# A Fourier transform feeding a mixture of experts: mirrored columns folded in the tables for five batches instead of three, and two batches' row tails written by VectorE

## The chip, the cores and the metric

The kernel runs on one core of a Trainium2 chip. The metric is the device time of one execution in microseconds (us). The kernel before has a median of 1130.99 us over three runs (1129.47 to 1132.53).

## The reference

The input x has 8 batches of 2496 rows with 256 features. The reference takes the Fourier transform over the rows and over the features and keeps the real part. Each of the 19968 resulting rows then goes to one of 8 experts:

```
X = np.fft.fft(x, axis=1);  X = np.fft.fft(X, axis=2);  x = X.real
logits = x @ w_gate;  e_idx = np.argmax(logits, axis=1)
gate_w = probs[np.arange(N), e_idx]              # softmax over the experts
eom = 1 / (1 + np.exp(-(x @ w_output_gate)))
for e in range(E):
    h = np.maximum(x[mask] @ w1[e], 0)           # 256 -> 1024
    out[mask] = gate_w * eom[mask, e] * (h @ w2[e])   # 1024 -> 256
```

So there is a transform of all batches, a gating decision per row, and two matrix products per row with the weights of its expert.

## The kernel before

**The transform of a batch.** A batch comes in five chunks of up to 128 columns (tiles `xt`, 128 x 8 x 128, fp32). `fold1` adds one half of a chunk to the other half (L416). For the batches from `LB` on it makes two more sums of the mirrored columns (L419, L420); for batches below `LB` it stops after L416, and the tables take that fold over. `fold2`, on VectorE (DVE), makes the tile `ft` (L431, L434, L443, L445). `dstage` multiplies a chunk with the first transform's tables, in fp32, for two parities: below `LB` as two accumulated products with 290 columns (L485), from `LB` on as three smaller products with 145, 80 and 145 columns (L487 to L489). `devac` rounds the result into the fp16 pair `ahi` and `alo` (ScalarE, ACT, at L497; DVE at L498). `sstage` is the second transform (fp16, L524), in five steps i for each batch; `sevac` adds and splits its result into `rows` (L546 to L559), tiles whose rows hold 256 features and two more words.

**Gating.** `gating(b)` picks the expert of each row and its place in a table in HBM, `scr`. It ends by writing two words, weight and place, behind the features of the rows: five small copies on ACT (L653). Then come 20 indirect DMAs (L657), issued by GpSimd (POOL), which scatter the rows into `scr`. They are woven in groups of five (`SPL`) between the chunks' folds.

**The experts.** They start when batches 0 and 1 have been scattered (`BA` = 2). A slot takes 256 rows of one expert: `load_x_` reads `scr` through a transposing DMA (L1105, tile `xr`) and a small DMA (L1106), both issued by SP; `conv` makes fp16 pairs of the weights (L1125, L1126); `mm1` and `mm2` are the two products (L1145 into `hp`, L1165 into `yp`); L1149 and L1150 evacuate `hp` into `hh` and `hl`; L1172 scales the result and L1173 (POOL) writes it out. The transform of the later batches runs in between.

**Who does fold1, and the order.** Chunks of batches 0 and 1 have their `fold1` on DVE, all others on POOL. SP and POOL run their instructions in the order in which the program is written; PE (TensorE), ACT and DVE in an order that a scheduler chose when the kernel was built. Each engine takes its queue strictly in order.

Of the kernel before, what the change touches and what calls it, by code (L numbers as in the profile page):

```python
# [12 lines left out]
I32 = mybir.dt.int32  # L13
# [4 lines left out]
NB, S, D, E, F = 8, 2496, 256, 8, 1024  # L18
# [16 lines left out]
RW = D + 2  # L35
# [6 lines left out]
BA = BAS[0]  # L42
# [28 lines left out]

AHEAD = (5, 6, 7, 8, 9), (4, 5, 6, 7, 8)

LB = BA + 1
PH1 = {mybir.EngineType.SP, mybir.EngineType.Pool}
BIG = float(1 << 20)

# [155 lines left out]
def fft_moe_kernel(ctx: ExitStack, tc: tile.TileContext, xl, wg, w1, w2, tde, tdo, gt, ts0, tsm, tsr, tsq, cst, tid, out):  # L233
    nc = tc.nc
# [43 lines left out]
    if True:  # L278
# [129 lines left out]
        def fold1(b, c, eng):  # L408
# [7 lines left out]
            eng.tensor_tensor(x0, x0, x1, op=ALU.add)  # L416
            if b < LB:
                return
# [3 lines left out]
        def fold2(b, c):  # L422
# [5 lines left out]
            ft = f[c] = pf.tile([128, 2, 2, 128], F32, name="ft", tag="ft", bufs=7)  # L428
            h = int(b >= LB)
            v = xts[b, c].rearrange("p (h a b) n -> p h a b n", h=2, a=2)[:, h]  # L430
# [45 lines left out]
        def dstage(b, c):  # L476
# [4 lines left out]
            for par in range(2):  # L481
                o = ps[W, par]
                if b < LB:
                    for k in range(2):
# [76 lines left out]
        def gating(b):  # L561
# [11 lines left out]
            def t3(name, shape=(128, 20, 8)):  # L573
                return pg.tile(list(shape), F32, name="r_" + name, tag="r_" + name, bufs=1)
# [70 lines left out]
            car = t3("car", (128, 20, 2))  # L645
# [4 lines left out]
            for i in range(5):  # L650
                r_ = s["rows"][i].rearrange("p a d w -> p (a d) w")
                rf.append(r_)
                nc.scalar.copy(r_[:, :, D:RW].bitcast(I32), car[:, 4 * i:4 * i + 4].bitcast(I32))  # L653
                yield

            def scatter(j):
# [326 lines left out]
        def steps():  # L983
            wk = 0
            fc = KC + 1
            for n in range(5 * NB):
                b, i = divmod(n, 5)
                if i == 0 and b > 0:
                    add_gen(gating(b - 1))
                    if b <= BA:  # L990
                        for ph in "CACC":
                            weave(piece(ph))
                    if b == BA:
                        first.append(table_a(0))
                        while next(first[0]) != "scales":
                            pass
# [30 lines left out]
                while wk <= 2 * E and wk < (n + 1) * (2 * E + 1) / WEND:  # L1027
# [5 lines left out]
                    wk += 1  # L1033
                yield ("step", n)
            add_gen(gating(NB - 1))
            while gens:
                for _ in piece("C"):
# [293 lines left out]
```

## Time and profile before

| what | value |
|---|---|
| median of the runs shown | 1130.99 us |
| the profiled execution: time, and its span | 1137.68 us, 1135.9 us |
| mean granted TensorE clock | 0.976 of full speed |
| PE busy | 1044.0 us (92% of the span) |
| DVE busy | 822.9 us (72%) |
| ACT busy | 732.4 us (64%) |
| POOL busy | 490.1 us (43%) |
| chain that ended last, by engine | PE 63%, POOL 9%, DVE 8%, issue 7%, ACT 7%, DMA 4% |

Busy shares are means over stages. The page's 40 slices (28.4 us each) show PE at 4 to 5 tenths in the third to sixth slice and at 9 or more almost everywhere from the twelfth on, while POOL is at 8 tenths in the fourth to sixth slice, its highest. So the stages must be read apart. The first number of a row of the timeline is its start within the span, the second how long it took; in brackets stands how long the engine idled before it and what ended that.

### The profile page before, as it was taken

The numbers are of one execution on the slowest core, as the hardware profiler recorded it, in microseconds if no ns is written. First come the engines' busy times: TensorE is split into PE (matmuls) and PEld (weight loads), VectorE is DVE, ScalarE is ACT, GpSimd is POOL, SyncE is SP. The second block draws the span as 40 slices with busy tenths as digits, with TensorE's granted clock in tenths as the row PEclk, the third lists the DMA queues.
The fourth block names the chain that finished last, engine by engine and source line by source line (L and its number), as shares of the span: only waits on it lengthen the run. The fifth ranks groups of instructions, "written<-read, shape, count | busy, mean of one in ns | idle before, by whom it ended". The sixth has DMA issues, their size and how long they took to land.

```text
span 1135.9 us, 28531 instructions
## 1 busy us (share of the span) xinstructions
PE 1044.0 (92%) x10060; PEld 932.3 (82%) x10060; DVE 822.9 (72%) x1516; ACT 732.4 (64%) x1224; POOL 490.1 (43%) x417
## 2 busy tenths in 40 slices
PE   5874559979889999999999999999999999999898
PEld 4664549869779899998888888899889989898787
DVE  6768877786988857578544545587788777787684
ACT  3887547656676655655445455677777776787584
POOL 0238874848848455463762122132222222322231
PEclk9998759989999999999999999999999999999999
DMA  9886545655558556667876424647667555565651
GB/s 369 318 312 232 216 122 180 176 157 162 164 147 187 154 135 164 157 170 184 208 195 167 109 57 140 177 136 176 163 168 200 133 167 126 140 183 137 182 131 30
DMA packets 158212, 194.08 MB, mean 171 GB/s; under 512 B 117885, under 2 KB 118527, under 8 KB 156020
## 3 DMA queue, kind: packets, MB, share of 16 engines
q1 hardware_dynamic: 142100, 149.68, 49.4%
q0 software_dynamic: 15824, 42.14, 11.2%
q8 instruction: 79, 1.29, 0.5%
q14 instruction: 65, 0.53, 0.2%
q10 hardware_dynamic: 144, 0.44, 0.1%
HBM read 193.47 MB, written 43.46 MB: 209 GB/s over the span
## 4 chain that ended last, share of the span: by engine, by line
PE 63%; POOL 9%; DVE 8%; issue 7%; ACT 7%; DMA 4%; SPq 2%; POOLq 0%; DVEq 0%; ACTq 0%
PE hp L1145 30%; PE yp L1165 29%; POOL scr L657 4%; PE psb_t L524 2%; POOL xt L416 2%; POOL out_dram L1173 2%; ACT wt L369 1%; DVE w1b L1126 1%; DVE w0b L1126 1%; DMA raw1b<-in_w_dram 1%; DVE hl L1150 1%; ACT w1b L1125 1%; DMA scr<-rows,desti 1%; DMA wt<-in_w_dram 1%; POOL xt L420 1%
## 5 line engine op out<-in xcount | busy, mean ns | idle before, releaser
L1145 PE MATMUL hp<-xr,w0b 128*128 128x256 f16 (+2 forms) x4224 | 484.2, 265 | 25.2 <-DVE hl L1150 18.6
L1165 PE MATMUL yp<-w1b,hh 128*128 128x256 f16 x2608 | 448.0, 273 | 3.7 <-DVE w1b L1126 2.1
L1145 PEld LDWEIGHTS <-w0b 128*128 128x128 f16 x4224 | 385.9, 98 | 76.1 <-issue 16.3
L1173 POOL DMA_INDIRECT out_dram<-y,xf x163 | 213.4, 1309 | 522.6 <-ACT y L1172 490.5
L1165 PE MATMUL yp<-w1b,hl 128*128 128x256 f16 (+3 forms) x1304 | 355.8, 273 | 0.0
L1165 PEld LDWEIGHTS <-hh 128*128 128x128 f16 x2608 | 251.5, 98 | 32.0 <-issue 3.9
L1149 ACT ACTIVATE hh<-hp 128x512 f16<-128x512 f32 (+4 forms) x352 | 193.9, 554 | 116.8 <-PE hp L1145 116.2
L1150 DVE SCALAR_TENSOR_TENSOR hl<-hp,hh 128x512 f16<-128x512 f32 (+4 forms) x352 | 222.4, 638 | 58.6 <-ACT hh L1149 57.8
L1126 DVE SCALAR_TENSOR_TENSOR w1b<-raw1b,ssc,w1b 128x1024 f16<-128x1024 f32 x144 | 188.0, 1307 | 104.1 <-ACT w1b L1125 104.1
L1126 DVE SCALAR_TENSOR_TENSOR w0b<-raw0b,ssc,w0b 128x1024 f16<-128x1024 f32 x144 | 188.4, 1311 | 63.2 <-ACT w0b L1125 60.7
L657 POOL DMA_INDIRECT scr<-rows,desti x160 | 183.7, 1148 | 67.7 <-issue 44.2
L1125 ACT ACTIVATE w0b<-raw0b,ssc 128x1024 f16<-128x1024 f32 x144 | 164.5, 1146 | 64.3 <-PE hp L1145 40.2
L1125 ACT ACTIVATE w1b<-raw1b,ssc 128x1024 f16<-128x1024 f32 x144 | 165.0, 1147 | 48.1 <-PE yp L1165 34.8
L1165 PEld LDWEIGHTS <-hl 128*128 128x128 f16 (+3 forms) x1304 | 127.8, 98 | 17.4 <-issue 2.5
L1172 ACT ACTIVATE y<-yp,ysc 128x256 f32<-128x256 f32 (+1 forms) x163 | 68.9, 470 | 47.8 <-PE yp L1165 41.7
L416 POOL TENSOR_TENSOR xt<-xt 128x500 f32<-128x500 f32 (+1 forms) x30 | 40.6, 1354 | 48.2 <-DMA xt<-in_xl_dram 27.2
L524 PE MATMUL psb_t<-ahi,tstq 125*128 125x145 f16 (+1 forms) x384 | 42.4, 230 | 0.3 <-DVE alo L498 0.3
L485 PE MATMUL psb_t<-tdet,ft 128*125 128x290 f32 (+1 forms) x120 | 34.4, 440 | 8.9 <-DVE alo L498 5.1
L524 PEld LDWEIGHTS <-tstq 125*128 125x128 f16 (+1 forms) x576 | 39.9, 99 | 1.9 <-issue 0.6
L487 PE MATMUL psb_t<-tdet,ft 128*125 128x145 f32 (+1 forms) x100 | 23.1, 315 | 17.1 <-DVE eo L548 10.6
L524 PE MATMUL psb_t<-alo,tstq 125*128 125x145 f16 (+1 forms) x192 | 38.6, 228 | 0.0
L555 DVE TENSOR_TENSOR rows<-rt,rows 128x516 f16<-128x516 f32 x40 | 31.5, 789 | 9.1 <-ACT rows L554 8.8
(213 smaller groups left out, 867.2 us busy)
## 6 DMA issues: line engine op xcount, KB each, us to landing
raw0b<-in_w_dram SPq DMA_DIRECT2D x144, 512.0 KB
raw1b<-in_w_dram SPq DMA_DIRECT2D x144, 512.0 KB
xt<-in_xl_dram SPq DMA_DIRECT2D x40, 512.0 KB
wt<-in_w_dram SPq DMA_DIRECT2D x16, 1024.0 KB
out_dram<-y,xf POOLq DMA_INDIRECT x163, 3.3
scr<-rows,desti POOLq DMA_INDIRECT x160, 4.9
xr<-scr SPq DMA_TRANSPOSE x88
xf<-scr SPq DMA_DIRECT2D x75, 2.0 KB
```

What stands on the lines that cost most here:

```text
L416: eng.tensor_tensor(x0, x0, x1, op=ALU.add)
L485: nc.tensor.matmul(o[:, 0:290], ft[:, k, par, W], tdab[:, k], start=(k == 0), stop=(k == 1))
L524: nc.tensor.matmul(ps[:, k, c0:c0 + 145], tab[hl][t][K], a[K, kc, par, c0:c0 + 145], start=(n == 0), stop=(n == len(terms) - 1))
L657: free_order("scr", batch=b, inst=nc.gpsimd.indirect_dma_start(out=scr[:, :], out_offset=bass.IndirectOffsetOnAxis(ap=desti[:, j:j + 1], a ...
L1125: nc.scalar.activation(w[:, 0], r, AF.Copy, scale=sc)
L1126: nc.vector.scalar_tensor_tensor(w[:, 1], r, sc, w[:, 0], op0=ALU.mult, op1=ALU.subtract)
L1145: nc.tensor.matmul(ps[:, k, T], w1v[:, hl, kc, (f % 4) * 128:(f % 4 + 1) * 128], a["x"][:, x, T], start=(m == 0), stop=(m == 5))
L1149: nc.scalar.activation(hh[:, G, T], ps[:, :, T], AF.Relu)
L1150: nc.vector.scalar_tensor_tensor(hl[:, G, T], ps[:, :, T], 0.0, hh[:, G, T], op0=ALU.max, op1=ALU.subtract)
L1165: nc.tensor.matmul(a["yp"][0:M, u], a[k, h][:, f, u * 128:u * 128 + M], w2v[:, hl, f], start=(g == 0 and f == 0 and m == 0), stop=(h == 1 ...
L1172: nc.scalar.activation(a["y"][0:M, u], a["yp"][0:M, u], AF.Copy, scale=ys[0:M, u:u + 1])
L1173: free_order("out", nc.gpsimd.indirect_dma_start(out=out[:, :], out_offset=bass.IndirectOffsetOnAxis(ap=a["f"].bitcast(I32)[0:M, u, 1:2], ...
```

## The change

`LB` goes from 3 to 5: `fold1` ends after L416 for batches 3 and 4 too, and their `dstage` takes the two products with 290 columns. In `gating`, for batches 0 and 1, the five copies of weight and place are made by DVE instead of ACT. Line numbers behind that place grow by 3 (L657 is L660 in the changed kernel, L1145 is L1148).

```
-LB = BA + 1
+LB = BA + 3
...
-                nc.scalar.copy(r_[:, :, D:RW].bitcast(I32), car[:, 4 * i:4 * i + 4].bitcast(I32))
+                if b < BA:
+                    nc.vector.tensor_copy(r_[:, :, D:RW].bitcast(I32), car[:, 4 * i:4 * i + 4].bitcast(I32))
+                else:
+                    nc.scalar.copy(r_[:, :, D:RW].bitcast(I32), car[:, 4 * i:4 * i + 4].bitcast(I32))
```

Place one, POOL, from the first scatters of batch 0 on (`xt` is a chunk, `scr` the table in HBM). Before:

```order
L657 DMA scr<-rows,desti 161024x258 x5
L416 TENSOR_TENSOR xt<-xt 128x4x125
L419 TENSOR_TENSOR xt<-xt 128x2x125
L420 TENSOR_TENSOR xt<-xt 128x2x125
L416 TENSOR_TENSOR xt<-xt 128x4x125
L419 TENSOR_TENSOR xt<-xt 128x2x125
L420 TENSOR_TENSOR xt<-xt 128x2x125
L657 DMA scr<-rows,desti 161024x258 x5
L416 TENSOR_TENSOR xt<-xt 128x4x125
```

Of the change, the same place on POOL:

```order
L660 DMA scr<-rows,desti 161024x258 x5
L416 TENSOR_TENSOR xt<-xt 128x4x125 x2
L660 DMA scr<-rows,desti 161024x258 x5
L416 TENSOR_TENSOR xt<-xt 128x4x125
L660 DMA scr<-rows,desti 161024x258 x5
```

The L419 and L420 of ten chunks are gone, eight of these chunks ahead of the last scatter of batch 1; nothing else of POOL's or SP's order is different.

Place two, DVE, where the gating of batch 0 ends (`r_car` holds weight and place, `alo` is the first transform's low half). Before:

```order
L647 SCALAR_TENSOR_TENSOR r_car<-r_se,p_x,r_num 128x20
L498 SCALAR_TENSOR_TENSOR alo<-psb_t,p_x,ahi 125x580 x2
L542 SCALAR_TENSOR_TENSOR rt<-psb_t,qb 128x2x129 x2
L555 TENSOR_TENSOR rows<-rt,rows 128x4x129
L498 SCALAR_TENSOR_TENSOR alo<-psb_t,p_x,ahi 125x580 x2
L548 SCALAR_TENSOR_TENSOR eo<-psb_t,qb 128x290 x2
L431 TENSOR_TENSOR ft<-xt 128x2x125
```

Of the change, the same place on DVE:

```order
L647 SCALAR_TENSOR_TENSOR r_car<-r_se,p_x,r_num 128x20
L498 SCALAR_TENSOR_TENSOR alo<-psb_t,p_x,ahi 125x580
L654 COPY rows<-r_car 128x4x2 x5
L498 SCALAR_TENSOR_TENSOR alo<-psb_t,p_x,ahi 125x580
L542 SCALAR_TENSOR_TENSOR rt<-psb_t,qb 128x2x129 x2
L555 TENSOR_TENSOR rows<-rt,rows 128x4x129
L498 SCALAR_TENSOR_TENSOR alo<-psb_t,p_x,ahi 125x580
L431 TENSOR_TENSOR ft<-xt 128x2x125
L434 TENSOR_TENSOR xt<-xt 128x2x125
L431 TENSOR_TENSOR ft<-xt 128x2x125
```

The five copies stand behind one L498, and the first fold of batch 3 (L431) stands earlier among the other work.

Place three, PE, just ahead of the experts' first product (`hp`). Before:

```order
L487 MATMUL psb_t<-tdet,ft 125x145
L488 MATMUL psb_t<-tdot,ft 125x80
L489 MATMUL psb_t<-tdot,ft 125x145
L600 MATMUL psm_t<-r_inc,cs 128x8
L601 MATMUL psm_t<-r_inc,cs 128x8
L1145 LDWEIGHTS w0b_1528
L1145 MATMUL hp<-xr,w0b_1528 128x256
```

Of the change, the same place on PE:

```order
L524 LDWEIGHTS tst_108
L524 MATMUL psb_t<-ahi,tst_108 128x145
L524 LDWEIGHTS tst_108
L524 MATMUL psb_t<-alo,tst_108 128x145
L1148 LDWEIGHTS w0b_1510
L1148 MATMUL hp<-xr,w0b_1510 128x256
```

The last 19 products (L524) of batch 3's first step, the first transform of two chunks of batch 4 and the two small products of batch 2's gating (L600, L601), which stood ahead of the experts' first 24 products, now stand behind them. On DVE, 24 instructions that stood ahead of the first L1150 stand behind it: two L548, two L552, two L555 and 18 of batch 2's gating.

## Rows read from the trace of the kernel before

**Rows 1.** Windows: stretch, length, busy PE, PEld, DVE, ACT, POOL; clock, DMA, GB/s

```profile
75.00:155.60 80.60, 43.76 (x407) 40.63 (x407) 60.90 (x163) 50.75 (x99) 69.03 (x64) 0.77 0.58 205
140.00:170.00 30.00, 14.77 (x75) 12.23 (x75) 22.15 (x57) 14.71 (x38) 22.87 (x21) 0.60 0.43 115
170.00:200.00 30.00, 30.00 (x305) 27.65 (x306) 22.60 (x37) 20.84 (x34) 14.03 (x12) 1.00 0.59 180
```

**Rows 2.** Chain that ended last, 140 to 182 us: start, length, what

```profile
161.29 3.55 DMA xf<-scr
```

**Rows 3.** Timeline of PE, 153 to 162 us: the experts' first product

```profile
160.55 1.87 PE L1145 MATMUL hp<-xr,w0b 128*128 128x256 f16 x8 [5.77 <-DMA xr<-scr]
```

**Rows 4.** Groups of POOL, 74 to 155.7 us: busy, mean ns | idle before

```profile
L657 POOL DMA_INDIRECT scr<-rows,desti x40 | 46.8, 1169 | 32.9 <-ACT rows L653 22.1 <-issue 10.2 <-ACT ahi L497 0.6
...
L420 POOL TENSOR_TENSOR xt<-xt 128x250 f32<-128x250 f32 (+1 forms) x8 | 6.4, 796 | 0.0
L419 POOL TENSOR_TENSOR xt<-xt 128x250 f32<-128x250 f32 (+1 forms) x8 | 6.3, 789 | 0.6
```

**Rows 5.** Timeline of POOL, 74 to 156 us

```profile
74.75 1.14 POOL L657 DMA_INDIRECT scr<-rows,desti  x1 [22.07 <-ACT rows L653]
...
82.36 0.72 POOL L419 TENSOR_TENSOR xt<-xt 128x250 f32<-128x250 f32 x1
...
104.50 1.27 POOL L416 TENSOR_TENSOR xt<-xt 128x500 f32<-128x500 f32 x1
...
117.61 1.17 POOL L657 DMA_INDIRECT scr<-rows,desti  x1 [0.16 <-issue]
...
154.63 0.99 POOL L657 DMA_INDIRECT scr<-rows,desti  x1 [0.30 <-issue]
```

**Rows 6.** Timeline of DVE, 70 to 101 us

```profile
70.45 0.23 DVE L647 SCALAR_TENSOR_TENSOR r_car<-r_se,p_x,r_num 128x20 f32<-128x20 f32 x1
70.60 1.55 DVE L498 SCALAR_TENSOR_TENSOR alo<-psb_t,p_x,ahi 125x580 f16<-125x580 f32 x2
...
93.70 0.33 DVE L585 SCALAR_TENSOR_TENSOR r_score<-r_dd,cs 128x160 f32<-128x160 f32 x1
...
100.67 0.23 DVE L647 SCALAR_TENSOR_TENSOR r_car<-r_se,p_x,r_num 128x20 f32<-128x20 f32 x1
100.82 0.17 DVE L754 CAST r_av<-r_pri 128x8 f32<-128x8 int32 x1
100.89 0.17 DVE L629 TENSOR_TENSOR desti<-r_dest,cs 128x20 int32<-128x20 f32 x1
```

**Rows 7.** Timeline of ACT, 74 to 75 us

```profile
74.25 0.61 ACT L653 COPY rows<-r_car 128x8 int32<-128x8 int32 x5
```

**Rows 8.** Timeline of PE, 33 to 94 us: first transform, both forms

```profile
33.69 4.13 PE L485 MATMUL psb_t<-tdet,ft 128*125 128x290 f32 x16
...
92.59 0.41 PE L487 MATMUL psb_t<-tdet,ft 128*125 128x145 f32 x2
...
93.30 0.41 PE L487 MATMUL psb_t<-tdet,ft 128*125 128x145 f32 x2
```

**Rows 9.** Chain that ended last, 322 to 330 us

```profile
324.32 1.91 PE psb_t L524 x30
```

**Rows 10.** Groups of DVE, 139 to 166 us

```profile
L555 DVE TENSOR_TENSOR rows<-rt,rows 128x516 f16<-128x516 f32 x4 | 4.5, 1127 | 0.0
L548 DVE SCALAR_TENSOR_TENSOR eo<-psb_t,qb 128x290 f32<-128x290 f32 x6 | 2.5, 452 | 0.0
L552 DVE TENSOR_TENSOR rt<-eo 128x258 f32<-128x258 f32 x6 | 2.3, 421 | 0.0
...
L633 DVE TENSOR_REDUCE r_se<-r_ex 128x20 f32<-128x160 f32 x1 | 0.3, 314 | 0.0
```

**Rows 11.** The tile rows: duration ns min/median/max, first and last start

```profile
L555 DVE TENSOR_TENSOR rows<-rt,rows x40: 685/694/2434, 37.2 to 502.9; 128x516 f16<-128x516 f32 x40
```

**Rows 12.** Groups of PE, 170 to 340 us

```profile
L1145 PE MATMUL hp<-xr,w0b 128*128 128x256 f16 x481 | 62.1, 279 | 12.6 <-DVE hl L1150 12.6
```

## The prediction

> **What bounds the kernel now.** I read the 40 slices first, then the windows, the chain of waits, and the timelines of POOL, DVE and PE. From 75 to 155.6 us PE works 43.8 of 80.6 us and POOL 69.0 [rows 1]. From 170 us on PE is busy all the time [rows 1]. So the kernel has a first part in which PE waits, and a second in which it is full; the first ends when the experts start. The reader is to find what starts them: their first product runs at 160.55, and PE had then idled 5.77 us for the tile `xr` out of `scr` [rows 3]. The chain shows why it is late: the last scatter of batch 1 is issued at 154.63, and the second of the small reads of `scr` only at 161.29 [rows 2, 5]. From the first scatter, at 74.75, to that last one POOL never idles for more than its own gaps: 40 scatters take 46.8 us, the gaps "issue" 10.2, and the folds the rest [rows 4]. POOL's queue sets the start of the experts, though POOL is the least used engine over the span.
>
> **Part one: fewer folds on POOL.** Of the ten chunks of batches 3 and 4, eight are folded ahead of the last scatter of batch 1. Their L419 and L420 go: 6.3 and 6.4 us busy [rows 4]. An L420 begins some hundredths before its L419 has ended in the rows, so I take 12.3 us for the eight pairs. All of it is on the path, since the queue is in order and the scatters stand behind. The other two chunks stand behind the last scatter: nothing.
>
> **Part two: the copies on DVE.** POOL idled 22.07 us until the first copy of weight and place was made on ACT [rows 5]. DVE had written `r_car` by 70.68 [rows 6], but ACT had other work queued ahead and began at 74.25 [rows 7]; the scatter followed 0.50 us behind. On DVE the copies stand behind one L498 (0.78, half of the 1.55 for two [rows 6]): they begin at 71.4, and the first scatter at 71.9, 2.8 us sooner. No copy of this form is on DVE in this trace. Its nearest row is the cast of 8 elements in a row, 0.17 us, with the next instruction 0.07 us behind [rows 6]: five copies cost DVE 0.35 to 0.85 us, ten 0.7 to 1.7. I take 0.1 each, 1 us. What waits behind them is the evacuation of the first transform, on which PE may wait; PE idles 37 us in this part, so I cost it at nothing, and at 1.7 us if that cover is gone. ACT loses ten copies, 1.2 us at 0.61 for five [rows 7], where it isn't the bound: nothing. For batch 1 the copies come at 101 already and are needed at 117.61 [rows 5, 6]: nothing, as long as that stays so (below).
>
> L555 on DVE takes 694 ns as a rule and 2434 at most [rows 11], and 1127 as a mean just before the start of the experts [rows 10]; POOL is busy 22.9 of 30 us there [rows 1]. The Trainium skill, "SBUF — State Buffer", section "Who interferes with whom", says that a DVE copy can take the port pair that DVE and GpSimd share, that the second to issue then blocks fully, and that GpSimd can't write descriptors meanwhile. ACT's copies never did that, so this rule speaks against part two: a scatter could wait for up to five copies, 0.85 us for each of two batches, and the sum below would be 1.7 us less gain. It also speaks for part one, as two-input DVE work blocks against POOL's folds; by it DVE would get back the 1.7 us or so of L555's longest. I take neither into the sum.
>
> **Start of the experts.** 12.3 + 2.8 = 15.1 us sooner: last scatter at 139.5, first product at 145.4.
>
> Something else could then be late. Batch 1's scatters now begin at 117.61; five of the eight pairs lie before that (7.7 us), so POOL would be there at 107.1. Its rows must be ready by then. In the new order DVE does the folds of chunks (3,0) to (3,3) before the main part of batch 1's gating, and each waits for POOL. The POOL fold of (3,3) ends at 105.77 now [rows 5]; less 2.8 and three pairs (4.6) that is 98.4. From L585 to `r_car` the gating took 7.0 us [rows 6], so the copies come at about 105.5 to 106.5. That is a margin of one microsecond: I take no wait, 0 and 6 as the ends.
>
> **Part three: what PE and DVE have to do later instead.** The folded tables cost PE more: a chunk takes 2.07 us (16 records, two chunks, in 4.13) against 1.42 for two parities of 0.71 [rows 8]. That is 0.65 a chunk, 3.3 us a batch. Batch 3's chunks run in the first part, where PE has room: nothing (3.3 if it hadn't). Batch 4's five run behind the start now, where PE is full: 3.3 us. Also moved behind the start are two of these chunks at the old price, 2 x 1.42 = 2.8; 19 products of the second transform at 0.064 (30 in 1.91 [rows 9]), 1.2; and the two small products of the gating, which I put at 0.6. Together 3.3 + 2.8 + 1.2 + 0.6 = 7.9 us that PE does at full load instead of while waiting.
>
> DVE gets 24 instructions behind the first L1150: two L548 and two L552, 0.87 each pair on average, two L555 at 0.69, eight gating steps of 160 elements at 0.31 and ten small ones at 0.17 [rows 6, 10, 11]. That is 1.7 + 1.4 + 2.5 + 1.7 = 7.3 us, or 11.9 if all are stretched like the mean of L555 in the crowded stretch before the start (1.13 against 0.69 [rows 10, 11]). DVE is busy 22.6 of 30 us behind the start [rows 1], and PE already idles 12.6 us for L1150 between 170 and 340 us [rows 12]. Most of the 7.3 lies beside the 7.9 that PE has to do itself. I add 1 us for the part that doesn't; bounds 0 and 11.9.
>
> **The sum.** -15.1 + 7.9 + 1.0 = -6.2 us. On the profiled execution's own time, 1137.68 (span 1135.9 and 1.8 around it), that is 1131.5. The median of the runs shown lies 6.7 us below the profiled time, so I forecast 1124.8, in round numbers 1125 us.
>
> **The rivals.**
>
> *More comes through.* PE's extra work fills holes that the second part has anyway, above all the 12.6 us of waiting for L1150 [rows 12], and DVE, freed of waits, keeps up. Then only batch 4's dearer tables count: -15.1 + 3.3 = -11.8, 1119 us. For it: the holes exist, and they are larger than what PE gets. Against it: those waits are for DVE, which gets work too.
>
> *The copies of batch 1 come too late.* The wait at the first scatter of batch 1 takes the place of the folds. With 6 us of it the gain is -15.1 + 6 + 7.9 + 1 = -0.2, 1131 us: no change. For it: the margin of 1 us, and DVE held by POOL's folds in the new order. Against it: part two starts everything sooner.
>
> *Slower: the experts starve on DVE.* The start comes sooner, but the moved DVE work stands in the queue ahead of the first L1150s, and PE has only two `hp` tiles to run ahead. If the stretched 11.9 us come one behind the other with PE's 7.9, the sum is -15.1 + 7.9 + 11.9 = +4.7, 1136 us. It decides from the point where PE's waits for L1150 grow by more than 7.2 us over today's 12.6. For it: DVE at 75% right behind the start and several POOL folds around it. Against it: DVE's work is mostly work that PE's own moved work waits for or lies beside.
>
> That the change doesn't do what it says is no rival: the order of POOL shows the instructions gone.
>
> **How the numbers follow.** The forecast's case has 0.52, with its own range of 1120 to 1129. More comes through: 0.20. Copies too late: 0.15. Starving: 0.13. About 0.3%, 3.4 us, is what a measurement can tell from no change. Faster by more than that is nearly all of the first two cases (0.46 + 0.20) and a little of the third, 0.67. Within it: 0.06 of the first, 0.13 of the third, 0.01 of the fourth, 0.20. Slower: 0.13. The range of 1116 to 1133 takes in the first case and the third, and the second without its far end; it leaves out the fourth and that end.
>
> **What would show it.** The first scatter at 72, the last at about 139.5 instead of 154.6 and the first product of the experts near 145.4 show parts one and two right. A POOL wait for DVE at the first scatter of batch 1, with 107 as its time, shows the third case beginning. Part three is right if PE's waits for L1150 up to 340 us stay within 3 us of 12.6, and PE's total rises by about 6.6 us (two batches of tables). The prediction is wrong if the first product starts as forecast and the time is still the same or higher: then the start wasn't what the end hung on.

## The result and the profile after

The changed kernel takes 1125.58 us (median of 20 runs, 1122.79 to 1130.94); the kernel before, run beside it, 1133.82 (1129.47 to 1138.22). The ratio is 0.9929, with a 95% interval of 0.9916 to 0.9942: 8.0 us faster, between 6.6 and 9.5. Forecast were 6.2 us less. The two profiled executions differ by more, 1137.68 against 1124.42: that of before was one of its slower ones, as a second profile of it shows below.

POOL's timeline of the changed kernel answers to [rows 5]:

```profile
72.52 1.14 POOL L660 DMA_INDIRECT scr<-rows,desti  x1 [19.66 <-DVE rows L654]
...
106.38 1.19 POOL L660 DMA_INDIRECT scr<-rows,desti  x1 [0.97 <-ACT r_car L646]
...
137.01 0.97 POOL L660 DMA_INDIRECT scr<-rows,desti  x1 [0.31 <-issue]
```

The first scatter comes 2.2 us sooner, batch 1's first 11.2 and the last 17.6. Batch 1's first scatter now waits 0.97 us for its rows, where before it had 0.16 [rows 5]. In the groups of POOL from 72 to 138 us, which answer to [rows 4], L419 and L420 are gone:

```profile
L660 POOL DMA_INDIRECT scr<-rows,desti x40 | 43.6, 1089 | 31.4 <-DVE rows L654 19.7 <-issue 7.7 <-ACT r_car L646 1.0
L416 POOL TENSOR_TENSOR xt<-xt 128x500 f32<-128x500 f32 (+1 forms) x9 | 11.4, 1274 | 0.1
```

The scatters took 43.6 us together, against 46.8 in [rows 4]. In the second profile of before they took 41.9, so their length differs from profile to profile, and a shortening by the change is not shown:

```profile
L657 POOL DMA_INDIRECT scr<-rows,desti x40 | 41.9, 1049 | 32.9 <-ACT rows L653 22.0 <-issue 10.2 <-ACT ahi L497 0.3
```

PE's timeline answers to [rows 3]: the first 24 products of the experts.

```profile
142.76 2.78 PE L1148 MATMUL hp<-xr,w0b 128*128 128x256 f16 x24 [1.21 <-DMA xr<-scr]
```

The windows answer to [rows 1] (stretch, length, busy PE, PEld, DVE, ACT, POOL; clock, DMA, GB/s):

```profile
75.00:155.60 80.60, 50.61 (x428) 43.42 (x427) 63.98 (x179) 53.09 (x99) 56.78 (x51) 0.83 0.74 247
140.00:170.00 30.00, 26.15 (x235) 22.52 (x234) 28.99 (x71) 20.97 (x45) 6.19 (x7) 0.96 0.67 181
170.00:200.00 30.00, 30.00 (x289) 26.43 (x287) 22.62 (x32) 20.38 (x34) 21.81 (x19) 1.00 0.67 168
```

PE is now busy 26.2 of the 30 us from 140 on, against 14.8 before, and DVE 29.0: right behind the new start DVE is full. The group that answers to [rows 12], PE from 170 to 340 us, waits less for DVE than before:

```profile
L1148 PE MATMUL hp<-xr,w0b 128*128 128x256 f16 x472 | 59.2, 275 | 7.9 <-DVE hl L1153 7.8
```

A second profile of the kernel before, on a chip of about the same speed (1130.88 us), gives these rows of POOL and PE:

```profile
75.07 1.14 POOL L657 DMA_INDIRECT scr<-rows,desti  x1 [22.03 <-ACT rows L653]
...
151.16 0.98 POOL L657 DMA_INDIRECT scr<-rows,desti  x1 [0.30 <-issue]
```

```profile
156.77 5.28 PE L1145 MATMUL hp<-xr,w0b 128*128 128x256 f16 x24 [5.48 <-DMA xr<-scr]
```

Here the last scatter and the first product lie 3.5 and 3.8 us ahead of [rows 3, 5]. A start read from one profile is thus good to some 4 us. The change brings the first product forward by 17.8 us against [rows 3] and by 14.0 against this second profile; forecast were 15.1. How much of that lasts is read from POOL's output DMAs (L1173, in the changed kernel L1176): number 0, number 10 and number 28, from the second profile of before and then from the changed kernel:

```profile
176.97 1.00 POOL L1173 DMA_INDIRECT out_dram<-y,xf  x1 [10.62 <-ACT y L1172]
...
273.33 1.50 POOL L1173 DMA_INDIRECT out_dram<-y,xf  x1 [0.30 <-ACT hh L1149]
...
410.99 0.97 POOL L1173 DMA_INDIRECT out_dram<-y,xf  x1 [6.56 <-ACT y L1172]
```

```profile
166.68 1.06 POOL L1176 DMA_INDIRECT out_dram<-y,xf  x1 [15.74 <-ACT y L1175]
...
265.03 0.98 POOL L1176 DMA_INDIRECT out_dram<-y,xf  x1 [0.31 <-ACT ahi L497]
...
402.15 0.97 POOL L1176 DMA_INDIRECT out_dram<-y,xf  x1 [6.56 <-ACT y L1175]
```

The lead is 14.0 us at the first product, 10.3 at the first output, 8.3 at number 10 and 8.8 at number 28. At the end of these two profiles it is 6.5. Against the first profile of before the four leads are 17.8, 13.9, 14.0 and 14.0, and 13.3 at the end. So nearly 4 us are given back up to the first output, and 0.5 to 4 more behind it.

### The profile page after: what moved, and what is told of

The parts are those of the page before. It is cut to its first block, busy times and chain, and to the rows that moved or that the text cites. A ratio compares the mean times of both kernels' runs of the same rounds, so it can differ in the third digit from the quotient of the medians.

```text
span 1122.7 us, 28442 instructions
## 1 busy us (share of the span) xinstructions
PE 1043.4 (93%) x10020; PEld 928.4 (83%) x10020; DVE 819.8 (73%) x1526; ACT 731.4 (65%) x1214; POOL 470.8 (42%) x397
## 4 chain that ended last, share of the span: by engine, by line
PE 67%; DVE 10%; issue 8%; POOL 6%; ACT 5%; DMA 3%; SPq 1%; POOLq 0%; DVEq 0%; ACTq 0%
PE hp L1148 31%; PE yp L1168 30%; PE psb_t L524 3%; POOL scr L660 2%; POOL out_dram L1176 2%; PE psb_t L485 2%; DVE w1b L1129 2%; POOL xt L416 1%; DMA raw1b<-in_w_dram 1%; ACT w1b L1128 1%; DVE hl L1153 1%; DVE ft L431 1%; ACT wt L369 1%; DVE xt L434 1%; DVE w0b L1129 1%
## 5 line engine op out<-in xcount | busy, mean ns | idle before, releaser
L1148 PE MATMUL hp<-xr,w0b 128*128 128x256 f16 (+2 forms) x4224 | 480.0, 263 | 20.3 <-DVE hl L1153 18.6
L1148 PEld LDWEIGHTS <-w0b 128*128 128x128 f16 x4224 | 383.7, 98 | 69.9 <-issue 14.0
L1176 POOL DMA_INDIRECT out_dram<-y,xf x163 | 214.0, 1313 | 527.7 <-ACT y L1175 495.5
L1153 DVE SCALAR_TENSOR_TENSOR hl<-hp,hh 128x512 f16<-128x512 f32 (+4 forms) x352 | 221.9, 637 | 58.8 <-ACT hh L1152 58.2
L660 POOL DMA_INDIRECT scr<-rows,desti x160 | 180.5, 1128 | 66.1 <-issue 42.0
L485 PE MATMUL psb_t<-tdet,ft 128*125 128x290 f32 (+1 forms) x200 | 57.6, 439 | 12.1 <-DVE alo L498 4.8
L416 POOL TENSOR_TENSOR xt<-xt 128x500 f32<-128x500 f32 (+1 forms) x30 | 40.5, 1357 | 51.5 <-DVE alo L498 26.4
L485 PEld LDWEIGHTS psb_t<-tdet,ft 128*125 128x125 f32 (+1 forms) x200 | 38.6, 202 | 24.8 <-issue 7.1
L524 PE MATMUL psb_t<-ahi,tstq 125*128 125x145 f16 (+1 forms) x384 | 43.1, 232 | 2.3 <-DVE alo L498 2.2
L524 PEld LDWEIGHTS <-tstq 125*128 125x128 f16 (+1 forms) x576 | 40.4, 100 | 4.4 <-issue 2.9
L431 DVE TENSOR_TENSOR ft<-xt 128x250 f32<-128x250 f32 (+1 forms) x40 | 17.4, 442 | 32.6 <-POOL xt L420 20.6
L524 PEld LDWEIGHTS <-tst 128*128 128x128 f16 (+1 forms) x384 | 27.8, 102 | 13.8 <-DVE eo L548 8.1
```

The costliest lines, as they stand in the source:

```text
L485: nc.tensor.matmul(o[:, 0:290], ft[:, k, par, W], tdab[:, k], start=(k == 0), stop=(k == 1))
L524: nc.tensor.matmul(ps[:, k, c0:c0 + 145], tab[hl][t][K], a[K, kc, par, c0:c0 + 145], start=(n == 0), stop=(n == len(terms) - 1))
L660: free_order("scr", batch=b, inst=nc.gpsimd.indirect_dma_start(out=scr[:, :], out_offset=bass.IndirectOffsetOnAxis(ap=desti[:, j:j + 1], a ...
L1148: nc.tensor.matmul(ps[:, k, T], w1v[:, hl, kc, (f % 4) * 128:(f % 4 + 1) * 128], a["x"][:, x, T], start=(m == 0), stop=(m == 5))
L1153: nc.vector.scalar_tensor_tensor(hl[:, G, T], ps[:, :, T], 0.0, hh[:, G, T], op0=ALU.max, op1=ALU.subtract)
L1176: free_order("out", nc.gpsimd.indirect_dma_start(out=out[:, :], out_offset=bass.IndirectOffsetOnAxis(ap=a["f"].bitcast(I32)[0:M, u, 1:2], ...
```

## The experiments

They ran on three chips: e1 to e4 on one, c, e6, e8 and e9 on the second, b and e10 to e12 on the third. On the first two the kernel before took 1159 to 1160 us, on the third 1134.06; each kernel is compared by its ratio to runs of before on its own chip. The profiles differ too: from 400 to 640 us PE is busy 224 to 227 of the 240 us on the first two, and all of them on the third and in the two profiles of the result. So what extra work costs on one of them need not be its price on another.

**Part one alone, and part two alone.**

```
e1:  LB = BA + 3, the copies all on ACT
e2:  LB = BA + 1, the copies of batches 0 and 1 on DVE
```

> Part one alone: LB at 5, the copies of weight and place stay on ACT. Theory (POOL's queue sets the start of the experts): the first scatter comes at 74.7 as before, the last one about 12 to 15 us sooner than 154.6, the first product of the experts near 146 to 148, and the time is 4 to 6 us below before (ratio about 0.995 to 0.997). Rival (the copies on DVE carry the gain): the time is that of before.

> Part two alone: LB stays 3, DVE makes the copies for batches 0 and 1. Theory: first scatter at 72 to 72.5, everything behind it 2 to 3 us sooner, first product at about 158, time 2 to 3 us below before (ratio about 0.998). Rival (the copies carry the gain): 7 to 8 us below before. Rival (DVE's copies hold up POOL's scatters): no gain or a loss.

Measured: e1 0.9939 (0.9916 to 0.9962), e2 1.0008 (0.9985 to 1.0032). The scatters of e1 (first, first of batch 1, last) and its first products:

```profile
76.54 1.14 POOL L657 DMA_INDIRECT scr<-rows,desti  x1 [21.99 <-ACT rows L653]
...
109.05 1.16 POOL L657 DMA_INDIRECT scr<-rows,desti  x1 [0.17 <-ACT rows L554]
...
138.43 0.97 POOL L657 DMA_INDIRECT scr<-rows,desti  x1 [0.31 <-issue]
```

```profile
144.05 2.78 PE L1145 MATMUL hp<-xr,w0b 128*128 128x256 f16 x24 [0.61 <-DMA xr<-scr]
```

And of e2, the first and the last scatter:

```profile
72.71 1.14 POOL L660 DMA_INDIRECT scr<-rows,desti  x1 [19.69 <-DVE rows L654]
...
151.82 1.62 POOL L660 DMA_INDIRECT scr<-rows,desti  x1 [0.30 <-issue]
```

Part one carries the gain: 7.1 us of 1159 (4.4 to 9.7), where 4 to 6 were expected. Part two does bring the first scatter forward: it comes at 74.75, 75.07 and 76.54 in the three profiles with the copies on ACT, and at 71.9 to 76.3, in the middle 72.7, in the eleven with them on DVE. But the last scatter of e2 lies between those of the two profiles of before, and the time shows no gain: the expected 2 to 3 us are outside the interval. In e2 the lead was still there at batch 1's first scatter (113.25, against 115.48 in the second profile of before); then batch 1's 20 scatters took 24.4 us instead of 21.7. The changed kernel has 4.0 us of lead over e1 at the first scatter and 1.4 at the last: 0.8 went into the longer wait for batch 1's rows (0.97 us against 0.17), 1.8 into longer scatters. What makes scatters longer in one profile than in another is not shown.

**POOL's time given back.**

```
-            if b < LB:
+            if b < LB and b not in (BA + 1, BA + 2):
                 return
```

> The changed kernel, but POOL still makes L419 and L420 for batches 3 and 4; nothing reads what they write. Theory: POOL's queue is as long as before, the last scatter is back to 2 to 3 us below 154.6, the first product near 158, and with the dearer tables behind the start (three chunks of batch 4, 2 us) the time is within 2 us of before: the gain is gone. Rival (the gain comes from the tables, the new order of PE and DVE, or the copies, not from POOL's time): it keeps 5 us or more of the 8.

Measured: 1.0013 (0.9994 to 1.0032). POOL's first and last scatter, and PE's first products:

```profile
71.91 1.13 POOL L660 DMA_INDIRECT scr<-rows,desti  x1 [19.68 <-DVE rows L654]
...
149.94 0.98 POOL L660 DMA_INDIRECT scr<-rows,desti  x1 [0.30 <-issue]
```

```profile
155.71 2.78 PE L1148 MATMUL hp<-xr,w0b 128*128 128x256 f16 x24 [1.20 <-DMA xr<-scr]
```

With the two operations back on POOL and everything else of the change in place, the start falls back by 13 us and the gain is gone. The first product stays 5.8 us behind the last scatter, in e3 as in the changed kernel. That settles the mechanism: POOL's time ahead of the last scatter sets the start, and the gain hangs on it. Two of the ten chunks put back stand behind that scatter, so a small part of the loss can be theirs.

**What the dearer tables cost.**

```
e4:  LB = BA + 1, fold1 returns for b < LB + 2     (copies on DVE)
e6:  LB = BA + 4
e8:  dstage of batch 4 (b == BA + 2):  for k in (0, 1, 0, 1)
c:   the changed kernel again, on the chip of e6, e8 and e9
```

> Copies on DVE, tables and products of batches 3 and 4 as before (LB 3), but L419 and L420 of these two batches are left out, so their mirrored columns are not folded and those rows are not the reference's. POOL's queue is as short as in the changed kernel, PE does the cheaper products. Theory: first product near 143 as in the changed kernel, and the time 2 to 4 us below the changed kernel's (PE saves 0.65 us for each chunk of batch 4 that stands behind the start), 10 to 12 us below before. Rival (the dearer products are hidden in PE's holes): the same time as the changed kernel.

> The changed kernel itself, beside the others of this call: ratio to before 0.993 again, first product of the experts near 143, and the experts' output DMAs 12 to 14 us sooner than before through the first 400 us.

> LB at 6: six batches folded in the tables. Theory: batch 5's folds stand on POOL behind the last scatter of batch 1, so the start of the experts stays near 143, and PE pays 3.3 us more for batch 5 at full load: 2 to 4 us above the changed kernel (ratio to before 0.995 to 0.997). Rival (POOL's folds bound the stretch from 170 to 340 us too, since the scatters and outputs queue behind them): as fast as the changed kernel or up to 5 us faster.

> The changed kernel, but PE makes the first transform's products of batch 4 twice (five chunks at 2.07 us, the second run overwriting the first). Theory: behind the start PE is the bound, so nearly all of it is paid: 7 to 10 us above the changed kernel, the gain over before gone. Rival (PE's holes behind the start hide such work, so the dearer tables are free): 0 to 3 us above the changed kernel.

Measured: e4 0.9926 (0.9901 to 0.9951), the changed kernel again 0.9929 (0.9902 to 0.9956), e6 0.9905 (0.9869 to 0.9942), e8 0.9949 (0.9929 to 0.9969). The cheaper products of e4 give nothing that shows over the changed kernel, which did not run on e4's chip. Nor is e4's profile clean on this: PE idled 5.1 us for DVE ahead of the experts, and their first product came 7.0 us behind the last scatter (138.66), against 5.8 in the changed kernel.

```profile
145.66 5.07 PE L1148 MATMUL hp<-xr,w0b 128*128 128x256 f16 x24 [5.14 <-DVE eo L548]
```

e8 is clean: 10.4 us more of PE's work behind the start cost 0.0020 of 1153.5, 2.3 us (-1.6 to 6.2, from the two intervals), outside the 7 to 10 that the theory wanted; the medians of e8 and of the repeat are the same to 0.01 us. e6, which should have been slower than the changed kernel, is not: its interval ends below the 0.995 expected at least. So PE's work behind the start is not paid in full on this chip, and the price that I had put on it is too high. The repeat of the changed kernel missed a part of what was expected: its first product came at 146.37, since its first scatter was at 76.26 instead of 72.52, in the same program. The starts of single profiles vary by that much. The 12 to 14 us expected for its outputs can't be read, as no profile of before is from this chip.

**Folds moved behind the scatters.**

```
-                while fc <= min(KC * (b + 1) + AHEAD[b >= BA][i], KC + 3 * n + 2):
+                while fc <= min(KC * (b + 1) + (5 if b == BA else AHEAD[b >= BA][i]), KC + 3 * n + 2):
```

> The changed kernel, with the folds of chunks (4,1) and (4,2) moved on POOL from ahead of the last scatters of batch 1 to behind them. Theory: the last scatter and the first product come 2.6 us sooner (first product near 140); as batch 4's work on DVE and PE then falls behind the start, at most half of it reaches the end: 0 to 2.5 us below the changed kernel. Rival (DVE, not POOL, sets the start by now): first product stays at 142 to 143 and the time is the same or above.

Measured: 0.9986 (0.9963 to 1.0010): the gain of the changed kernel is nearly lost. The last scatter, SP's reads and PE's first products:

```profile
133.19 0.97 POOL L660 DMA_INDIRECT scr<-rows,desti  x1 [0.30 <-issue]
```

```profile
140.40 2.11 SPq L1122 DMA_DIRECT2D raw0b<-in_w_dram  x2
143.31 1.34 SPq L1108 DMA_TRANSPOSE xr<-scr  x1
```

```profile
149.94 3.81 PE L1148 MATMUL hp<-xr,w0b 128*128 128x256 f16 x24
```

POOL was done 3.8 us sooner, and yet the read of `scr` came 3.9 us later than in the changed kernel (139.44): in SP's queue it stands behind a weight load, which waited for DVE's conversion. But DVE had itself waited for others just before:

```profile
136.82 0.83 DVE L548 SCALAR_TENSOR_TENSOR eo<-psb_t,qb 128x290 f32<-128x290 f32 x2 [6.47 <-ACT qb L546]
```

And the instruction of DVE right ahead of that conversion (L722, 1.61 us instead of 0.26) lasted until POOL's moved folds were done, at 139.05. In this profile PE had a stretch from 124 to 134 us with about half a microsecond of "issue" ahead of most matmuls. The first product, at 149.94, is where neither the theory nor the rival put it. So the loss is measured; whether DVE sets the start, as the rival says, and how much of the loss is the moved folds', is open.

**What bounds the stretch behind the start.**

```
e10: L431 of batch 5 (b == BA + 3) made seven times
e11: L420 of batch 5 made four times
e12: LB = BA + 6
```

> The kernel before itself, one look, for its trace beside those of the others on this chip: first scatter at 74 to 77, last at 154 to 157, first product of the experts at 160 to 163.

> The changed kernel, but DVE makes the first subtraction of each chunk of batch 5 seven times (30 times more, some 0.33 us each, 10 us), all of it behind the start of the experts. If DVE is the bound there: 6 to 10 us above the changed kernel. If it isn't (as doubling PE's work of batch 4 cost only 2 of its 10 us): 0 to 3 us above.

> The changed kernel, but POOL makes L420 four times for each chunk of batch 5 (15 times more, 0.7 us each, 10.5 us), behind the start of the experts. If POOL's queue bounds the stretch behind the start, as the look at six folded batches suggests: 5 to 10 us above the changed kernel. If it isn't the bound there: 0 to 3 us above.

> All eight batches folded in the tables. Against six: POOL loses 20 more of its operations (14 us) between 200 and 340 us, PE gets 2 x 3.3 us more. If POOL's queue bounds that stretch: equal to six or up to 4 us faster. If PE does: 3 to 6 us slower than six, ratio to before 0.993 to 0.996.

Measured: e10 0.9983 (0.9964 to 1.0002), e11 0.9964 (0.9947 to 0.9981), e12 0.9890 (0.9867 to 0.9913). The changed kernel's 0.9929 is the result's, beside a kernel before of much the same time (1133.82 against 1134.06). Against it 10 us more of DVE cost 6.1 us (3.5 to 8.7), 10.5 us more of POOL 4.0 (1.6 to 6.4), and 10.4 us more of PE, above, 2.3. The 6.1 of e10 lies at the lower end of what was expected if DVE is the bound, and e11's 4.0 between its two expectations. None of the three doses is paid in full, so none of the engines is the bound alone; which is the nearest to it is not shown, as the intervals overlap and e8 is from another chip. A part of it can be seen in the waits of the changed kernel from 140 to 340 us (total, times, longest):

```profile
DVE ft L431 <- POOL xt L420: 19.3, 8, 3.8
```

DVE waits for POOL's folds, and PE for DVE. Taking L419 and L420 off POOL for all batches (e12) has the lowest ratio: 12.5 us below before (9.9 to 15.1), and 4.4 below the changed kernel (1.4 to 7.4); from e6's ratio it differs by less than the noise. Its windows from 140 to 340 us, under those of the changed kernel:

```profile
140.00:340.00 200.00, 181.27 (x1757) 161.57 (x1756) 169.33 (x354) 134.17 (x256) 127.48 (x110) 0.99 0.59 163
```

```profile
140.00:340.00 200.00, 189.23 (x1772) 165.65 (x1770) 169.41 (x358) 138.24 (x260) 111.00 (x89) 0.99 0.61 170
```

POOL has 16 us less to do and PE is busy 8 us more in the same 200.

## Why the prediction was right, and where not

**What bounds the kernel:** right, and shown by e3. PE's holes ahead of the experts were POOL's queue. Two readings on the way to it were off. The small read at 161.29 lies behind the first product and can't have made it late; what did is that SP's first read of `scr` (L1105) starts as the last scatter lands:

```profile
154.63 2.44 DMA scr<-rows,desti
157.08 1.34 SPq L1105
```

And of the slices, PE's at 4 to 5 tenths are the fourth to sixth; the third is at 7. POOL is at 8, 8 and 7 tenths there.

**Part one, 12.3 us:** right in kind. e1 shows it alone: from the first to the last scatter 61.9 us, against 79.9 and 76.1 in the two profiles of before, so 14 to 18 instead of 12.3. The scatters make 5.0 us of the 18 (41.8 us in e1, 46.8 in [rows 4]) and nothing of the 14 (41.9 in the second profile), so the removed folds account for some 13 to 14.

**Part two, 2.8 us:** about 2.2 us at the first scatter, nothing that shows at the end (e2; and e1 is as fast as the whole change within the intervals). The copies cost DVE 0.45 us for five, inside the 0.35 to 0.85. By the Trainium skill, "SBUF — State Buffer", section "Who interferes with whom", a DVE copy can hold GpSimd off. These copies can't show a price of that: no scatter runs beside either five, from 71.44 to 71.89 and from 105.45 to 105.90, since POOL then waits for them.

**The wait at batch 1's first scatter:** taken as none, with 107 us as POOL's time there. POOL came at 105.4 and waited 0.97 us, until 106.38; 2.13 in e6. The row names ACT's L646, but that copy itself waited for L654; what the scatter needs are DVE's five copies (L654). The margin was as thin as read, and what used it up was an instruction of DVE ahead of the copies, which lasted until a fold of POOL had ended:

```profile
103.57 1.89 DVE L709 COPY r_deada<-r_g 128x12 f32<-128x12 f32 x1
105.45 0.45 DVE L654 COPY rows<-r_car 128x8 int32<-128x8 int32 x5
```

```profile
104.13 1.28 POOL L416 TENSOR_TENSOR xt<-xt 128x512 f32<-128x512 f32 x1
```

In the repeat L709 took 0.16 us, and L782 was the one that lasted until L416's end (106.83 to 108.71, 1.88 us instead of 0.17). Without the 1.7 us the copies would have been done before POOL came, by my estimate. That DVE and POOL hold each other up was seen in the prediction and left out of its sum.

**Part three:** the step that failed in its sizes. PE's 7.9 us of dearer and moved products were priced in full, DVE's 7.3 us of moved work at 1. e8 shows that PE's work there is not paid in full (2.3 of 10.4 us, at most 6.2), and e10 that DVE's is not nearly free (6.1 of 10, at least 3.5). With the two shares as measured, 7.9 and 7.3 become 1.7 and 4.5, 6.2 us; but the intervals are wide and from two chips, so that DVE's work is the dearer of the two is likely and not shown. Forecast was -15.1 + 8.9. Measured by the two profiles of before, the start came 17.8 and 14.0 us sooner and the end 13.3 and 6.5, so 4.5 and 7.5 us were given back. The total came out right because the two errors have opposite signs, which is luck. So is the closeness of 1124.8 to 1125.58: the forecast started from a median of three runs, 1130.99, and that of the twenty is 1133.82; the gain was 8.0 where 6.2 were forecast. The rise of PE's busy time by 6.6 us can't be seen: it is 1044.0 and 1048.1 in the two profiles of before and 1043.4 in the changed kernel, and L1145's own fell from 484.2 to 480.0.

**The rivals:** waits for L1150 did not grow but fall (12.6 us, in the second profile of before 11.3, to 7.8), so the experts did not starve from 170 us on. That is also more than the 3 us by which they were to stay near 12.6 if part three was right. DVE full from 140 to 170 us may be that rival's beginning, and the 4 us lost up to the first output its price; this is argued, not shown. "More comes through" did not happen with five batches. With eight the gain is as large as that rival's; POOL's relief behind the start, which I hadn't counted at all, fits that, as e11 shows that POOL's work there has a price.

## What to carry to other kernels

An engine that is little used over the span can still set the start of the main work: read its queue in the stretch where the bound engine idles, and count everything that stands ahead of the one instruction that others wait for. Where several engines hand work to one another, price moved work by what a dose of it costs on the chip, not by which engine shows 100%: PE, the busiest one, took 10.4 us more for 2.3 (at most 6.2). Where two engines share the work on a chunk, check whether an instruction of the one lasts until the other's has ended: here that made five copies late, and the scatters behind them. A single profile can be 4 us off at one event; take two before a difference of that size is explained.

## What the runs showed of the hardware

The experts' first 24 products take 2.78 us in the changed kernel and 5.28 in both profiles of before. The windows of just these stretches, of the changed kernel and of the first profile of before, give the granted clock as 1.00 and 0.50 of full speed (the sixth figure behind the length), 2.4 and 1.2 GHz:

```profile
142.70:145.60 2.90, 2.84 (x28) 2.56 (x28) 2.90 (x11) 2.27 (x7) 0.00 (x0) 1.00 0.70 104
```

```profile
160.50:165.80 5.30, 5.25 (x25) 3.75 (x25) 3.67 (x13) 2.71 (x11) 1.28 (x2) 0.50 0.75 205
```

PE had idled 1.21 us ahead of the first and 5.77 us ahead of the second; ahead of the 1.21 it had run 29 of batch 3's products. That is 2.5 us that no term of the sum held; counted from the end of these products, 2.5 us more are given back behind them. It is not sure to come: the repeat of the changed kernel took 4.87 us for the same 24, after 1.16 us of idling.

While POOL's fold L416 runs, some instructions of DVE last until it ends and some do not. In the changed kernel L431 took 1.45 us (as a rule 0.42), L709 1.89 (0.17) and, beside two folds at the start of the experts, L555 3.33 (0.69); they ended 0.05 to 0.6 us behind the fold. L1153 kept its 0.68 us beside a fold, and L459 its 0.14.
